# Windowed attention with a top-128 expert: ranking products at the ends of steps, loads two tiles ahead, weights a step later, batch entry behind the last turn

## The chip, the core and the metric

The kernel runs on one core of a Trainium2 chip. The time is the device time of one execution in microseconds; shown are the median of the runs and the smallest and largest of them. One execution more is taken with the hardware profiler, and all rows below are of that one.

## What is computed

Eight batches of 576 tokens go through attention with 8 heads of 64, where a token sees itself and the 63 tokens before it. The result, 512 wide, then goes through one expert per batch: the 128 tokens with the highest gate score are taken, go through two matrix products (512 to 1024 to 512), are scaled by the sigmoid of their score and added to the output at their places. The reference, cut:

```python
scores = scale * np.matmul(q, k.transpose(0, 1, 3, 2))     # 8 batches, 8 heads, S=576, D=64
mask = (rel >= 0) & (rel < 64)
scores = np.where(mask, scores, -1000000000.0)
...
x = attn @ v                                               # as (8, 576, 512)
gate = np.einsum('bsd,d->bs', x, w_gate)
out = x.copy()
for b in range(8):
    top_idx = np.argpartition(-gate[b], 128)[:128]
    xe = x[b, top_idx]
    ye = np.maximum(xe @ w1, 0.0) @ w2
    out[b, top_idx] = x[b, top_idx] + 1 / (1 + np.exp(-gate[b, top_idx])) * ye
```

All matrix products are made in full float32 for the attention, and for the expert from a high and a low part of each operand (three products: high by high, low by high, high by low), so that a product is as exact as float32.

## The kernel before

**Steps.** The 72 windows of 64 tokens (9 for each batch) are worked in 36 tiles of two windows. One step of the main loop (L690) works on several tiles at once: it issues the loads of tile n+3 (`AHEAD`), the store of tile n-3, the scores of tile n (TensorE, L264, tiles `s`), the values of tile n-2 (TensorE, L310, `av`), the maxima of tile n (VectorE, L276) and its exponentials (ScalarE, L284, `p`, first half), the transposes of tile n-1 (TensorE, L292, `t`) with their copies into `pt` (ScalarE, L294), the second half of the exponentials, and the output and gate dot of tile n-2 (VectorE, L319 to L322 and L237, `x` and `jk`; the dot lands in one column of `scores`). Each engine works off its instructions in the order in which they are written, so the order of the code is the order of the work.

**The expert stream.** `moe()` is a generator that issues one expert product or so each time it is asked. A step asks it `QUANTA` = 8 times, behind all of the step's attention. It goes through the batches in groups, (0), (1), (2), (3), (4, 5), (6, 7). For a single batch: `moe_in` transposes the 128 gathered rows `xe` (TensorE, `xt`, L501) and splits them into `xh` and `xl` (ScalarE copies, VectorE subtracts, L226 and L227); 24 products N=512 against `w1` give `hp` (L581) in two halves; the halves `n` are turned (TensorE, `ht`, L557; turn 0 and turn 1) and split into `hh` and `hl`; 24 products against `w2` give `yp` (L632), which is scaled, added (L638) and scattered by an indirect DMA on GpSimd's queue (L641). A pair has its products N=256 in the other orientation (`hp` L598) and no turn. While `yp` of a batch is being made the next group may enter: at column c in `ENTER` = (3, 6), if the rows have been gathered (L620). When the attention is through, a tail loop (L736) asks the stream `TAILQ` = 6 times behind each point of the ranking.

**The ranking.** `choose(b)` is a generator for each batch that a step advances at named points (`step_chain`). It transposes the gate scores of the batch's tiles into rows (`r`, TensorE, L409; the first four tiles as one part, the fifth as the other), copies the row (ScalarE, L413), counts for each token how many are larger (VectorE, five compares, `cmp`, L421), sums up where the chosen ones go (`lo`, 15 products N=1, L446), makes `diff` (L455), selects by slot (`sel`, L462: five instructions on GpSimd, on VectorE for the batches 0 and 7, which are called urgent), and sums up the indices (`ix`, five products, L471). `fx` and `idx` (VectorE, L475 and L477) and an indirect DMA (L479) gather the rows. The points of a step were, in this order: F, scores, values, P, maxima and first exponentials, S, R, transposes, output and gate, V, expert stream, E.

**Buffers in PSUM.** Two for the scores (`ps_s`), two for the transposes `t`, and for `r`, `lo` and `ix` as well (`ps_t`), one for the values, two for the expert stream's `hp`, `ht`, `yp` and `xt` (`ps_m`). In the tail the stream takes from `ps_t` too, once no ranking is left.

**Weights.** The 16 pieces of `w1` and `w2` are loaded by `load_w` in the steps of `PIECES`, and split into high and low on GpSimd (L207, L209) `WLAG` = 3 steps later, behind the step's V point. **Dummy products.** `keep_warm` (L95, `kw`) puts groups of four 64-wide products on zeros behind the scores of steps 0 to 2, 8, 6 and 3 groups.

Of the kernel before, what the change touches and what calls it, by code (L numbers as in the profile page):

```python
# [24 lines left out]
AHEAD = 3  # L25
# [7 lines left out]
KEEP = {0: 8, 1: 6, 2: 3}  # L33
# [3 lines left out]
PIECES = {n: 1 for n in range(2, 10)} | {10: 2, 11: 1, 12: 2, 13: 2, 14: 1}  # L37
WLAG = 3
# [3 lines left out]
ENTER = (3, 6)  # L42
# [7 lines left out]
def tile_attention_moe(ctx: ExitStack, tc, q, k, v, wg, w1, w2, outs, B, H, S, D, C):  # L50
# [44 lines left out]
    def keep_warm(groups):  # L95

        d = [ps_m.tile([P, 512], F32, tag="x", name=f"kw{r}_{njunk[1]}") for r in range(2)]
        njunk[1] += 1
        for i in range(groups):
            for r, c in ((0, 0), (1, 1), (0, 1), (1, 0)):  # L100
                rs = slice(r * W, (r + 1) * W)
                nc.tensor.matmul(d[r][c * W:(c + 1) * W, :D1], warm[rs, c * W:(c + 1) * W],
                                 warm[rs, :D1], start=True, stop=True)

# [240 lines left out]
    closed = set()  # L347
# [46 lines left out]
    def choose(b):  # L394
# [31 lines left out]
        for part, (t0, t1) in enumerate(CUT):  # L426
            yield "P"
            while (b, part) not in closed:
                yield "P"
            yield from spread(t0, t1)  # L430
            if urgent:
                yield "V"
                for t in range(t1):
                    compare(t, t0 * P, min(end, t1 * P), part)
# [5 lines left out]
        yield "P"  # L440

# [15 lines left out]
        for t, (_, r, lo, _) in enumerate(segs):  # L457
# [4 lines left out]
            (nc.vector if urgent else nc.gpsimd).tensor_scalar(  # L462
# [3 lines left out]
        yield "E" if urgent else "P"  # L466
        while b - 4 >= scattered[0]:
            yield "P"
# [47 lines left out]
    def moe():  # L516
        for gi, group in enumerate(GROUPS):
# [94 lines left out]
            for u, b in enumerate(group):  # L612
# [4 lines left out]
                for c in range(KC2):  # L617
                    if ng == 1 and c == 4:
                        yield from turn_done(1)
                    if c in ENTER and u == ng - 1 and gi + 1 < len(GROUPS):  # L620
                        nxt = [x for x in GROUPS[gi + 1] if x not in entered]
                        if nxt and is_ready(nxt[0]):
                            moe_in(gi + 1, GROUPS[gi + 1].index(nxt[0]))
                            yield
                            yield
# [28 lines left out]
    load_v(0)  # L654
    load_v(1)
    load_q(2)
    load_k(2)
    nc.sync.dma_start(wgb, wg)
    load_v(2)
# [30 lines left out]
    for n in range(NM + 3):  # L690
# [7 lines left out]
        if 0 <= n - 3 < NM:  # L698
            attn_store(n - 3)
        step_chain("F")  # L700
        if n < NM:
# [5 lines left out]
        step_chain("P")  # L707
# [3 lines left out]
        step_chain("S")  # L711
        step_chain("R")
# [5 lines left out]
        if 0 <= n - 2 < NM:  # L718
            attn_out(n - 2)
            attn_gate(n - 2)  # L720
            for b in range(B):
                for part, (_, t1) in enumerate(CUT):
                    if SEG[b][t1 - 1][0] == n - 2:
                        closed.add((b, part))
# [11 lines left out]
    while chains or not done:  # L736
        slot += 1
        for kind in ("F", "P", "S", "R", "V", "E"):
# [40 lines left out]
```

## Time and profile before

| what | value |
|---|---|
| time, median of 3 runs | 279.59 us (277.85 to 279.79) |
| profiled execution | 277.96 us |
| its span, from first to last instruction | 276.15 us |
| mean granted clock of TensorE | 0.967 |
| busy: TensorE, VectorE, ScalarE, GpSimd | 238.1, 186.5, 152.7, 80.9 us |
| DMA, mean | 171 GB/s |

An engine that is busy for the whole span would have 276 us in the third row from below. The granted clock is the share of full speed that the chip gave TensorE. In a list of waits, "PE t L292 <- ACT row L413" means that TensorE stood idle in front of the product on line 292 that writes `t`, until ScalarE had ended the instruction on line 413 that writes `row`.

### The profile page before, as it was taken

The page shows a single profiled execution, that of the slowest core. Times are in us where ns is not written, and L with a number is a line of the kernel's source. Part 1 is how long each engine was busy: PE and PEld are TensorE (multiplying, and loading weights), DVE is VectorE, ACT ScalarE, POOL GpSimd, SP SyncE. Part 2 cuts the span into 40 slices and gives each one's busy share as a digit, 9 for nine tenths or more (in the row PEclk, how much of TensorE's full clock was granted, in tenths as well). Part 3 has the DMA queues.
Part 4 walks back from the last instruction along what each step waited for, and adds up shares of the span by engine and source line. Part 5 has one row for each costly group of instructions (what it writes and reads, how often), then busy time and mean ns, then how long its engine had stood idle before and what let it go on. Part 6 is the DMA issues. An engine that isn't in the chain of part 4 may idle for free.

```text
span 276.1 us, 11136 instructions
## 1 busy us (share of the span) xinstructions
PE 238.1 (86%) x4512; PEld 202.8 (73%) x4512; DVE 186.5 (68%) x959; ACT 152.7 (55%) x423; POOL 80.9 (29%) x123
## 2 busy tenths in 40 slices
PE   8885879879978898977979994999898799999992
PEld 8774668768765786766758883887686699879981
DVE  1596999999958896895638878495499744423321
ACT  2886777958766577683537876365668201122200
POOL 7225302970398515100520050105300520111011
PEclk9999988999999999995999999799999979999999
DMA  6999896997865387373556665262311220111011
GB/s 215 397 354 350 271 327 216 330 395 250 278 170 188 135 246 237 123 226 116 174 171 196 195 229 193 59 211 81 78 40 45 76 68 10 38 40 38 0 40 38
DMA packets 25156, 47.27 MB, mean 171 GB/s; under 512 B 2961, under 2 KB 3985, under 8 KB 25105
## 3 DMA queue, kind: packets, MB, share of 16 engines
q1 hardware_dynamic: 23680, 42.10, 46.0%
q0 software_dynamic: 1280, 4.20, 4.5%
q8 instruction: 36, 0.59, 0.9%
q10 hardware_dynamic: 144, 0.26, 0.3%
q14 instruction: 16, 0.12, 0.2%
HBM read 35.01 MB, written 11.53 MB: 169 GB/s over the span
## 4 chain that ended last, share of the span: by engine, by line
PE 46%; issue 17%; DVE 16%; ACT 13%; POOL 6%; POOLq 0%; ACTq 0%; DVEq 0%
PE s L264 10%; PE t L292 10%; PE av L310 8%; ACT p L284 7%; PE yp L632 6%; PE hp L581 5%; DVE p L276 5%; PE hp L598 3%; ACT pt L294 3%; DVE jk L237 2%; DVE x L322 2%; DVE cmp L421 2%; POOL sel L462 2%; DVE hl L227 1%; PE wp L93 1%
## 5 line engine op out<-in xcount | busy, mean ns | idle before, releaser
L284 ACT ACTIVATE p<-p,nm 128x128 f32<-128x128 f32 x288 | 91.7, 392 | 42.6 <-DVE nm L276 41.1
L276 DVE CUSTOM_DVE_ANT_0 p<-s,mask 128x128 f32<-128x128 f32 x288 | 63.5, 285 | 26.8 <-PE s L264 24.1
L292 PE MATMUL t<-ident,p 128*128 128x128 f32 x288 | 42.1, 281 | 13.1 <-ACT row L413 9.6
L310 PE MATMUL av<-v,pt 64*64 64x65 f32 x2176 | 44.7, 226 | 7.1 <-issue 5.9
L294 ACT COPY pt<-t 128x512 f32<-128x512 f32 x72 | 40.0, 583 | 19.1 <-PE t L292 18.9
L310 PEld LDWEIGHTS av<-v,pt 64*64 64x64 f32 x2176 | 42.2, 140 | 9.3 <-issue 7.3
L292 PEld LDWEIGHTS t<-ident,p 128*128 128x128 f32 x288 | 31.1, 141 | 19.3 <-ACT row L413 12.1
L264 PE MATMUL s<-k,q 64*64 64x128 f32 x1152 | 43.3, 286 | 1.3 <-DVE nm L276 0.5
L264 PEld LDWEIGHTS s<-k,q 64*64 64x64 f32 x1152 | 33.7, 139 | 12.6 <-issue 11.4
L462 POOL TENSOR_SCALAR sel<-slots,diff 128x128 bf16<-128x128 f32 x24 | 18.5, 781 | 40.2 <-DVE z L319 39.5
L237 DVE CUSTOM_DVE_ANT_0 jk<-x,wgb 128x512 bf16<-128x512 f32 x36 | 28.4, 789 | 1.2
L632 PE MATMUL yp<-w2h,hh 128*128 128x512 f32 x64 | 27.5, 430 | 0.3 <-POOL w2h L207 0.3
L632 PE MATMUL yp<-w2l,hh 128*128 128x512 f32 x64 | 26.2, 410 | 1.2 <-POOL w2l L209 1.2
L632 PE MATMUL yp<-w2h,hl 128*128 128x512 f32 x64 | 26.2, 410 | 0.0
L421 DVE SCALAR_TENSOR_TENSOR cmp<-row,scores,later 128x128 bf16<-128x128 f32 (+12 forms) x48 | 25.4, 561 | 0.5 <-ACT row L413 0.4
L322 DVE TENSOR_TENSOR x<-av,z 128x512 f32<-128x512 f32 x36 | 24.9, 691 | 1.2
L641 POOL DMA_INDIRECT out_dram<-xe,idx x8 | 8.2, 1020 | 58.6 <-DVE xe L638 48.1
L276 DVE DVE_READ_ACCUMULATOR2_ANT nm<- 128x1 f32 x288 | 23.7, 82 | 0.0
L479 POOL DMA_INDIRECT xe<-out_dram,idx x8 | 8.3, 1038 | 45.7 <-DVE nm L276 24.5
L598 PE MATMUL hp<-xh,w1l 128*128 128x256 f32 x64 | 18.4, 288 | 0.0
L598 PE MATMUL hp<-xh,w1h 128*128 128x256 f32 x64 | 18.3, 286 | 0.0
L598 PE MATMUL hp<-xl,w1h 128*128 128x256 f32 x64 | 18.3, 286 | 0.0
(84 smaller groups left out, 324.5 us busy)
## 6 DMA issues: line engine op xcount, KB each, us to landing
v<-in_v SPq DMA_DIRECT2D x36, 260.0 KB, 3.6
q<-in_q SPq DMA_DIRECT2D x36, 256.0 KB, 4.0
out_dram<-x SPq DMA_DIRECT2D x32, 256.0 KB, 2.8
k<-in_k SPq DMA_DIRECT2D x31, 256.0 KB, 4.2
st<-in_w SPq DMA_DIRECT2D x16, 256.0 KB, 4.6
k<-in_k SPq DMA_DIRECT2D x8, 128.0 KB, 3.2
out_dram<-x SPq DMA_DIRECT2D x8, 128.0 KB, 2.4
k<-in_k ACTq DMA_DIRECT2D x1, 256.0 KB
```

Source lines behind the costliest of these rows:

```text
L237: nc.vector.tensor_tensor_reduce(out=junk()[:n, :E], in0=xf[:n], in1=wgb[:n], op0=ALU.mult, op1=ALU.add, scale=1.0, scalar=0.0, accum_out=acc)
L264: nc.tensor.matmul(s[r][c * W:(c + 1) * W, j], Q[m][rs, j, c], keys(m, c, j, rs), start=True, stop=True)
L276: nc.vector.tensor_tensor_reduce(out=pe[:, j, :, r], in0=s[r][:, j], in1=mk, op0=ALU.add, op1=ALU.min, scale=-SCALE, scalar=3.0e38, accum_ ...
L284: nc.scalar.activation(pe[:, j, :, r], pe[:, j, :, r], AF.Exp, bias=nm[:, r, j:j + 1], scale=-1.0)
L292: nc.tensor.transpose(t[:, j, :], pe[:, j, a].rearrange("p r w -> p (r w)"), ident)
L294: nc.scalar.copy(pt, t)
L310: nc.tensor.matmul(av[cs, r, j * D1:(j + 1) * D1], pt[a][rs, j, cs], V[g // 2][rs, g % 2, j], start=a == 0 or o == c, stop=a == 1)
L322: nc.vector.tensor_tensor(out=x.rearrange("p j r d -> p r j d"), in0=av[:, :, :, :D], in1=z[:, 1].unsqueeze(3).to_broadcast([P, 2, NP, D]) ...
L421: nc.vector.scalar_tensor_tensor(out=above[t][r, c0:c1], in0=row[r, c0:c1], scalar=scores[r, m:m + 1], in1=later[r, c0 - a:c1 - a], op0=AL ...
L462: (nc.vector if urgent else nc.gpsimd).tensor_scalar(out=sel[r], in0=slots[r], scalar1=diff[r, t:t + 1], scalar2=float(lo - r.start), op0= ...
L598: nc.tensor.matmul(hp[:, j], w[:, c, js], a[:, c].rearrange("p u c -> p (u c)"), start=(n == 0), stop=(n == 3 * KC1 - 1))
L632: nc.tensor.matmul(yp[:C, :E], a[:, c % per, us], w[:, c, :], start=(n == 0), stop=(n == 3 * KC2 - 1))
```

## The change

- `r`, `lo` and `ix` are written at E, behind a step's expert products, and no more at P, ahead of its transposes. A part is taken only when its last gate dot was written in an earlier step (`closed` now holds the step). Their readers (row copy at R, indices at F, selections at S) stand first in the next step, ahead of its scores. Batches that are not urgent wait at one V more between the last compare and `lo`.
- The selections of batch 1 go from GpSimd to VectorE.
- Loads run two tiles ahead, no more three; `wgb` is loaded between the values of tiles 0 and 1.
- `keep_warm(n)` issues one product of n times 128 columns, n = 2, 2, 1 in the steps 0 to 2, in place of 32, 24 and 12 small ones.
- The weights' first piece is loaded in step 3, no more in 2, and split two steps later, no more three. The loads end in step 15.
- The next group enters at any column from 3 on, but behind a single batch only when both turns were made in an earlier block (a block is one step's share of the stream).
- The tail loop has R ahead, and no P.

```diff
-AHEAD = 3
+AHEAD = 2
...
-KEEP = {0: 8, 1: 6, 2: 3}
-PIECES = {n: 1 for n in range(2, 10)} | {10: 2, 11: 1, 12: 2, 13: 2, 14: 1}
-WLAG = 3
+KEEP = {0: 2, 1: 2, 2: 1}
+PIECES = {n: 1 for n in range(3, 16)} | {9: 2, 13: 2, 14: 2}
+WLAG = 2
...
-ENTER = (3, 6)
+ENTER = (3, 4, 5, 6, 7)
...
-    def keep_warm(groups):
-        d = [ps_m.tile([P, 512], F32, tag="x", name=f"kw{r}_{njunk[1]}") for r in range(2)]
+    def keep_warm(n):
+        d = ps_m.tile([P, 512], F32, tag="x", name=f"kw{njunk[1]}")
         njunk[1] += 1
...
+        nc.tensor.matmul(d[:, :n * P], warm, warm.unsqueeze(1).to_broadcast([P, n, P]),
+                         start=True, stop=True)
...
         for part, (t0, t1) in enumerate(CUT):
-            yield "P"
-            while (b, part) not in closed:
-                yield "P"
+            yield "E"
+            while (b, part) not in closed or closed[b, part] >= slot:
+                yield "E"
             yield from spread(t0, t1)
...
                 compare(t, 0, end, 0)
-        yield "P"
+            yield "V"
+        yield "E"
...
-            (nc.vector if urgent else nc.gpsimd).tensor_scalar(
+            (nc.vector if urgent or b == 1 else nc.gpsimd).tensor_scalar(
...
-        yield "E" if urgent else "P"
+        yield "E"
         while b - 4 >= scattered[0]:
-            yield "P"
+            yield "E"
...
-                    if c in ENTER and u == ng - 1 and gi + 1 < len(GROUPS):
+                    if (c in ENTER and u == ng - 1 and gi + 1 < len(GROUPS)
+                            and (ng > 1 or len(turned) == 2 and turned[1] < block[0])):
...
+    nc.sync.dma_start(wgb, wg)
     load_v(1)
-    load_q(2)
-    load_k(2)
-    nc.sync.dma_start(wgb, wg)
-    load_v(2)
...
+        step_chain("R")
         step_chain("F")
+        step_chain("S")
         if n < NM:
             attn_scores(n)
...
-        step_chain("P")
         if n < NM:
             attn_max(n)
             attn_exp(n, 0)
-        step_chain("S")
-        step_chain("R")
...
-                        closed.add((b, part))
+                        closed[b, part] = n
...
-        for kind in ("F", "P", "S", "R", "V", "E"):
+        for kind in ("R", "F", "S", "V", "E"):
```

The change moves instructions on every engine. Three places show how. A row is a line of the code, what it does, what it writes and what it reads; the number behind a name is the buffer.

**The ranking of batch 3 in step 19.** On TensorE before, `r3_0`, the transposed gate scores of the first four tiles of batch 3, stood ahead of the step's transposes `t18`, and batch 1's expert products behind these:

```order
L409 MATMUL r3_0_2390<-ident_162,scores_184 128x128 x4
L292 MATMUL t18_0_2421<-ident_162,p18_2264 128x128 x4
L292 MATMUL t18_1_2428<-ident_162,p18_2264 128x128 x4
L581 MATMUL hp1_0_2306<-w1h_186,xl1_2199 128x512
L581 MATMUL hp1_0_2306<-w1h_186,xh1_2198 128x512
L581 MATMUL hp1_0_2306<-w1l_187,xh1_2198 128x512
```

After, the transposes stand earlier in the step, and `r3_0` behind the last of its eight expert products, right ahead of the scores of step 20:

```order
L575 MATMUL hp1_0_2329<-w1h_186,xl1_2218 128x512
L575 MATMUL hp1_0_2329<-w1h_186,xh1_2217 128x512
L575 MATMUL hp1_0_2329<-w1l_187,xh1_2217 128x512
L403 MATMUL r3_0_2338<-ident_162,scores_184 128x128 x4
L258 MATMUL s20_0_2352<-k4_1867,q20_2117 64x128
L258 MATMUL s20_1_2353<-k4_1867,q20_2117 64x128
```

On ScalarE before, at the ranking of batch 4 in step 24, the row copy stood between the first half of the step's exponentials (`p24`, four of them) and the copies `pt23` of the transposes:

```order
L284 ACTIVATE p24_3003<-p24_3003,nm24_3004 128x2x64 x4
L413 COPY row4_2933<-r4_0_2998 128x512
L294 COPY pt23_0_3023<-t23_0_3018 128x512
L294 COPY pt23_1_3030<-t23_1_3025 128x512
L284 ACTIVATE p24_3003<-p24_3003,nm24_3004 128x2x64 x4
```

After, it stands ahead of the step's exponentials, which are those of tile 25 there, behind the last of the step before and its split of batch 2's rows:

```order
L278 ACTIVATE p24_2876<-p24_2876,nm24_2877 128x2x64 x4
L220 CAST xh2_2915<-xt2_2917 128x512
L407 COPY row4_2810<-r4_0_2946 128x512
L278 ACTIVATE p25_3022<-p25_3022,nm25_3023 128x2x64 x4
L288 COPY pt24_0_3041<-t24_0_3036 128x512
L288 COPY pt24_1_3048<-t24_1_3043 128x512
L278 ACTIVATE p25_3022<-p25_3022,nm25_3023 128x2x64 x4
```

**The entry of batch 2.** On TensorE before, in step 22, `ht1_1` (the second turn of batch 1) and `xt2` (the entry of batch 2) stood in one step with three products between them:

```order
L292 MATMUL t21_0_2762<-ident_162,p21_2634 128x128 x4
L292 MATMUL t21_1_2769<-ident_162,p21_2634 128x128 x4
L557 MATMUL ht1_1_2788<-ident_162,n1_1_2677 128x128 x4
L632 MATMUL yp1_2684<-w2h_188,hh1_0_2561 128x512
L632 MATMUL yp1_2684<-w2l_189,hh1_0_2561 128x512
L632 MATMUL yp1_2684<-w2h_188,hl1_0_2562 128x512
L501 MATMUL xt2_2802<-ident_162,xe2_2581 128x128 x4
L632 MATMUL yp1_2684<-w2h_188,hh1_0_2561 128x512
```

After, the turn stands in step 22, behind its transposes,

```order
L286 MATMUL t22_0_2785<-ident_162,p22_2657 128x128 x4
L286 MATMUL t22_1_2792<-ident_162,p22_2657 128x128 x4
L551 MATMUL ht1_1_2812<-ident_162,n1_1_2700 128x128 x4
L627 MATMUL yp1_2707<-w2h_188,hh1_0_2578 128x512
L627 MATMUL yp1_2707<-w2l_189,hh1_0_2578 128x512
```

and the entry in step 23, behind that step's transposes, with all of the step's attention between the two:

```order
L286 MATMUL t23_0_2890<-ident_162,p23_2771 128x128 x4
L286 MATMUL t23_1_2897<-ident_162,p23_2771 128x128 x4
L495 MATMUL xt2_2917<-ident_162,xe2_2604 128x128 x4
L627 MATMUL yp1_2707<-w2h_188,hh1_1_2817 128x512
L627 MATMUL yp1_2707<-w2l_189,hh1_1_2817 128x512
L627 MATMUL yp1_2707<-w2h_188,hl1_1_2818 128x512
```

**The tail.** On TensorE before, in step 36, the entry of batch 4 stood behind the transposes and three products of batch 3's `yp`; the second turn of batch 3, `ht3_1`, had come a step earlier:

```order
L292 MATMUL t35_1_4393<-ident_162,p35_4295 128x128 x4
L632 MATMUL yp3_4336<-w2h_188,hh3_0_4228 128x512
L632 MATMUL yp3_4336<-w2l_189,hh3_0_4228 128x512
L632 MATMUL yp3_4336<-w2h_188,hl3_0_4229 128x512
L501 MATMUL xt4_4414<-ident_162,xe4_3671 128x128 x4
```

After, the second turn comes behind the values of tile 35; `r7_0` and the entry of batch 4 follow four products later, and the entry of batch 5 three products behind that:

```order
L551 MATMUL ht3_1_4375<-ident_162,n3_1_4317 128x128 x4
L627 MATMUL yp3_4324<-w2h_188,hl3_0_4250 128x512
L627 MATMUL yp3_4324<-w2h_188,hh3_0_4249 128x512
L627 MATMUL yp3_4324<-w2l_189,hh3_0_4249 128x512
L627 MATMUL yp3_4324<-w2h_188,hl3_0_4250 128x512
L403 MATMUL r7_0_4388<-ident_162,scores_184 128x128 x4
L495 MATMUL xt4_4401<-ident_162,xe4_3685 128x128 x4
L627 MATMUL yp3_4324<-w2h_188,hh3_1_4380 128x512
L627 MATMUL yp3_4324<-w2l_189,hh3_1_4380 128x512
L627 MATMUL yp3_4324<-w2h_188,hl3_1_4381 128x512
L495 MATMUL xt5_4411<-ident_162,xe5_4150 128x128 x4
```

On VectorE before, the split of that turn (`hl3_1`) stood ahead of the output and gate dot (`x34`, `jk39`) of the last tile but one:

```order
L237 ISA jk38_4332,scores_184<-x33_4328,wgb_185 128x512
L237 ISA scores_184 128x1
L421 SCALAR_TENSOR_TENSOR cmp0_2_200,cnt2_194<-row6_4005,scores_184,later_167 128x320
L421 SCALAR_TENSOR_TENSOR cmp0_3_201,cnt2_194<-row6_4005,scores_184,later_167 128x192
L227 TENSOR_TENSOR hl3_1_4343<-ht3_1_4337,hh3_1_4342 128x512
L319 TENSOR_SCALAR z34_4400<-av34_4353 128x8
L321 RECIPROCAL z34_4400<-z34_4400 128x8
L322 TENSOR_TENSOR x34_4401<-av34_4353,z34_4400 128x2x4x64
L237 ISA jk39_4405,scores_184<-x34_4401,wgb_185 128x512
L237 ISA scores_184 128x1
L421 SCALAR_TENSOR_TENSOR cmp0_4_202,cnt2_194<-row6_4005,scores_184,later_167 64x64
L227 TENSOR_TENSOR xl4_4413<-xt4_4414,xh4_4412 128x4x128
```

After, it stands behind the output and gate dot (`x35`, `jk40`) of the last tile, and four compares of batch 7 stand between it and the splits of the two entries:

```order
L315 RECIPROCAL z35_4367<-z35_4367 128x8
L316 TENSOR_TENSOR x35_4368<-av35_4334,z35_4367 128x2x4x64
L231 ISA jk40_4372,scores_184<-x35_4368,wgb_185 128x512
L231 ISA scores_184 128x1
L415 SCALAR_TENSOR_TENSOR cmp0_4_202,cnt2_194<-row6_3890,scores_184,later_167 64x64
L221 TENSOR_TENSOR hl3_1_4381<-ht3_1_4375,hh3_1_4380 128x512
L415 SCALAR_TENSOR_TENSOR cmp1_0_203,cnt3_196<-row7_4314,scores_184,later_167 64x448
L415 SCALAR_TENSOR_TENSOR cmp1_1_204,cnt3_196<-row7_4314,scores_184,later_167 128x384
L415 SCALAR_TENSOR_TENSOR cmp1_2_205,cnt3_196<-row7_4314,scores_184,later_167 128x256
L415 SCALAR_TENSOR_TENSOR cmp1_3_206,cnt3_196<-row7_4314,scores_184,later_167 128x128
L221 TENSOR_TENSOR xl4_4400<-xt4_4401,xh4_4399 128x4x128
L221 TENSOR_TENSOR xl4_4400<-xt5_4411,xh4_4399 128x4x128
```

## Rows read from the trace of the kernel before

**Rows 1.** The page, busy time of TensorE with its share of the span, and the granted clock in 40 slices (tenths of full speed).

```profile
PE 238.1 (86%) x4512; PEld 202.8 (73%) x4512; DVE 186.5 (68%) x959; ACT 152.7 (55%) x423; POOL 80.9 (29%) x123
PEclk9999988999999999995999999799999979999999
```

**Rows 2.** The chain that ended last, in order of time, over steps 12 and 13: start in us, length in us, engine, what.

```profile
60.60 1.03 PE s L264 x32
61.64 0.93 PE av L310 x64
62.57 1.02 PE t L292 x8
63.59 1.86 PE hp L581 x8
65.45 1.03 PE s L264 x32
```

**Rows 3.** Windows over the whole span, cut where step 0, step 10, step 35, the first product of the pair (4, 5) and the end of TensorE's work (270.87) lie: window, its length, then busy us (and number) of TensorE, its weight loads, VectorE, ScalarE, GpSimd; granted clock, DMA share, GB/s.

```profile
4.82:47.84 43.02, 34.61 (x1035) 30.68 (x1034) 34.73 (x219) 31.93 (x94) 12.84 (x34) 0.96 0.93 320
47.84:204.14 156.30, 136.27 (x2847) 112.83 (x2847) 118.44 (x625) 103.05 (x288) 53.59 (x58) 0.97 0.59 190
204.14:222.61 18.47, 15.79 (x303) 13.30 (x303) 16.09 (x68) 8.73 (x22) 3.91 (x5) 0.94 0.16 59
222.61:270.87 48.26, 47.70 (x317) 42.50 (x315) 16.30 (x47) 7.73 (x20) 5.95 (x6) 0.99 0.10 34
```

**Rows 4.** TensorE's waits between 48 and 204 us: engine, instruction and line that waited, <- the releaser; us in total, times, longest.

```profile
PE t L292 <- ACT row L413: 7.0, 9, 1.7
PE xt L501 <- DVE hl L227: 5.7, 2, 3.3
PE t L292 <- ACT pt L294: 2.9, 4, 0.7
PE yp L632 <- POOL w2l L209: 1.2, 1, 1.2
```

**Rows 5.** Windows over steps 3 to 5, steps 6 to 9, and step 12 alone, columns as in rows 3.

```profile
15.35:29.64 14.29, 9.83 (x313) 8.70 (x313) 11.36 (x64) 10.25 (x31) 6.75 (x7) 1.00 1.00 335
29.64:47.84 18.20, 15.41 (x427) 13.63 (x426) 17.68 (x106) 14.22 (x42) 2.28 (x2) 0.91 0.82 275
60.53:65.38 4.85, 4.85 (x113) 4.15 (x113) 4.73 (x24) 2.81 (x10) 0.46 (x1) 1.00 0.84 286
```

**Rows 6.** TensorE's waits between 0 and 48 us, and the dummy products (durations in ns, smallest, median, longest; first and last start).

```profile
PE av L310 <- issue: 4.5, 3, 2.7
PE t L292 <- ACT row L413: 2.6, 2, 1.7
...
L102 PE MATMUL kw<-warm x136: 216/218/253, 6.0 to 13.2; 64*64 64x65 f32 x136
```

**Rows 7.** The chain in step 24, where a ranking product stands ahead of the transposes.

```profile
135.91 1.28 ACT p L284 x4
137.20 0.59 ACT row L413
...
137.84 0.67 PE t L292 x4
```

**Rows 8.** The selections, by engine: durations in ns, smallest, median, longest; first and last start.

```profile
L462 POOL TENSOR_SCALAR sel<-slots,diff x24: 712/718/1328, 74.5 to 218.2; 128x128 bf16<-128x128 f32 x24
L462 DVE TENSOR_SCALAR sel<-slots,diff x8: 278/284/288, 43.4 to 229.4; 128x128 bf16<-128x128 f32 x8
```

**Rows 9.** VectorE's gate dots over all tiles (times, busy us, mean ns), then rows of VectorE's timeline: one gate dot, and compares of the last batch (start, length, line, tiles).

```profile
L237 DVE CUSTOM_DVE_ANT_0 jk<-x,wgb 128x512 bf16<-128x512 f32 x36 | 28.4, 789 | 1.2
...
53.38 1.56 DVE L237 CUSTOM_DVE_ANT_0 jk<-x,wgb 128x512 bf16<-128x512 f32 x1
...
217.72 0.69 DVE L421 SCALAR_TENSOR_TENSOR cmp<-row,scores,later 64x448 bf16<-64x448 f32 x1
...
219.39 0.36 DVE L421 SCALAR_TENSOR_TENSOR cmp<-row,scores,later 128x128 bf16<-128x128 f32 x1
...
221.96 0.35 DVE L421 SCALAR_TENSOR_TENSOR cmp<-row,scores,later 128x128 bf16<-128x128 f32 x1
```

**Rows 10.** The entry of batch 2 in step 22, rows of the timeline (start, length; in brackets the idle time of the engine before), and windows over step 22, step 23 and step 29, columns as in rows 3.

```profile
125.13 0.69 DVE L227 TENSOR_TENSOR hl<-ht,hh 128x512 fp32r<-128x512 f32 x1 [0.49 <-ACT hh L226]
125.88 1.12 PE L501 MATMUL xt<-ident,xe 128*128 128x128 f32 x4 [3.28 <-DVE hl L227]
...
118.41:127.35 8.94, 5.66 (x117) 4.68 (x117) 6.51 (x34) 5.73 (x17) 0.00 (x0) 0.86 0.70 231
127.35:134.43 7.08, 7.08 (x129) 6.32 (x128) 4.43 (x23) 3.75 (x11) 2.32 (x4) 0.69 0.25 78
164.63:175.06 10.43, 6.71 (x107) 5.15 (x106) 6.59 (x29) 5.47 (x16) 1.26 (x2) 0.89 0.42 148
```

**Rows 11.** TensorE's timeline at the entry of batches 6 and 7, and TensorE's waits behind step 35's start.

```profile
242.92 0.60 PE L501 MATMUL xt<-ident,xe 128*128 128x128 f32 x4
...
246.18 0.63 PE L501 MATMUL xt<-ident,xe 128*128 128x128 f32 x4 [0.56 <-issue]
...
PE ix L471 <- POOL sel L462: 0.9, 2, 0.5
PE ix L471 <- POOL selh L462: 0.8, 1, 0.8
```

More of the change, by code (lines that the diff above doesn't have):

```diff
@@ L93, in tile_attention_moe @@
         nc.tensor.matmul(wp[:, j % NP], warm, warm, start=True, stop=True)
-    def keep_warm(groups):
-        d = [ps_m.tile([P, 512], F32, tag="x", name=f"kw{r}_{njunk[1]}") for r in range(2)]
+    def keep_warm(n):
+        d = ps_m.tile([P, 512], F32, tag="x", name=f"kw{njunk[1]}")
         njunk[1] += 1
[L99 to L103, printed above, removed]
+        nc.tensor.matmul(d[:, :n * P], warm, warm.unsqueeze(1).to_broadcast([P, n, P]),
+                         start=True, stop=True)
     FILL = -1e9 / SCALE
@@ L346, in tile_attention_moe @@
     scattered = [0]
-    closed = set()
+    closed = {}
     def segments(b):
```

## The prediction

> **What bounds the kernel now.** I read the page first: TensorE is busy for 238.1 us of a span of 276.1, far more than any other engine, and its clock stands below full in a few slices [rows 1]. Then I read the chain over two steps in which nothing is late: one step repeats after 4.85 us (60.60 to 65.45), and all of it is TensorE: scores 1.03, values 0.93, transposes 1.02, eight expert products 1.86 [rows 2]. So 2.98 us of attention and 0.233 us for each N=512 product are the prices, and a step that takes longer has a wait in it. Third, I cut the span where steps begin [rows 3]: the start (4.82 to 47.84, steps 0 to 9) takes 43.02 us, the middle (steps 10 to 34) 156.30 with TensorE busy for 136.27, the last attention step with all up to the first product of the pair (4, 5) 18.47 with 15.79 busy, the paired products 48.26 with 47.70 busy; from there to the end of the span, 276.15, it is 5.28. The middle holds 20.0 us of idle TensorE, which the list of its waits names almost whole [rows 4]: transposes behind the ranking's row copy 7.0, and 2.9 behind the `pt` copy that the first wait delays; the entry of a batch behind a split 5.7; `yp` behind weight splits 1.2. The start has other limits: VectorE is busy for 17.68 of the 18.20 us of steps 6 to 9 [rows 5], and its largest TensorE wait, 4.5 us before `av`, shows no releaser [rows 6].
>
> **The ranking products.** Before, `r` stands in front of a step's transposes, and it takes one of the two `ps_t` buffers that they need. Its reader, the row copy on ScalarE, stands behind the four exponentials: exponentials from 135.91, row copy at 137.20, transposes only at 137.84 [rows 7]. In the change `r`, `lo` and `ix` follow the step's expert products, and the readers are the first in the next step, ahead of exponentials and maxima. The next transposes come 1.96 us into the step (scores and values), and the row copy is by then done. I take back the 7.0 and the 2.9 of the middle whole: a step without ranking waits for nothing there. The waits in the start (2.6 us) [rows 6] I count at nothing, since VectorE is full there.
>
> What is added: `lo`, `ix` and `r` now stand ahead of the next scores, so a late one holds the step's scores, and VectorE and ScalarE behind these. `r` needs a gate dot of the step before and no more than a `pt` copy's buffer. `lo` has a free step behind the last compare, but for batches 0 and 7. `ix` waits for five selections on GpSimd, begun at the step's start: five at the median 0.718 are 3.6 us, at the longest 1.328 6.6 us [rows 8], against 4.7 us of TensorE work ahead of `ix`. I take 1.0 for the four batches in the middle (bounds 0 and 4 times 1.9). Batch 0's `lo` waits for compares of the same step: scores 9 start after VectorE has ended step 8, which leaves it idle for `lo` and what the selections don't cover; I take 1.0 of bounds 0 and 3.
>
> **Batch 1's selections** go from GpSimd to VectorE: 5 at 0.284 for batches 0 and 7 [rows 8], 1.4 us in step 16, where TensorE has 5.2 us of work; on the path nothing. VectorE does run longer beside GpSimd: a gate dot took 1.56 us at 53.38 against a mean of 0.789 [rows 9], so up to twice the 1.4. [...]
>
> **Entry behind the last turn.** In steps 22 and 29 the next batch's transposes `xt` follow the turn `ht` in the same step and need its PSUM buffer, so TensorE waits until ScalarE and then VectorE (125.13) have split it, to 125.88 [rows 10]: 5.7 us in two places. The change lets a batch enter only in a later step, after 3 us of that step's attention, when the split is done. Behind both waits the granted clock falls: 0.86 over 8.94 us, 0.69 over the next 7.08, 0.89 over 10.43 [rows 10]. At half speed these are 2.5, 4.4 and 2.3 us, together 9.2, of which about 1.0 idle; the busy rest costs half, 4.1 us. I take 5.7 and 4.1 (below: 5.7 alone).
>
> **Weights a step later.** The first use is a step later too (the expert stream starts in step 12 and no more in 11), and w2's pieces are split one step ahead of their product; GpSimd is rid of batch 1's selections. I take the 1.2 us [rows 4].
>
> **Two tiles ahead, fewer dummy products.** The 136 records of `kw` end at 13.2 us [rows 6]; nothing but tiles that VectorE holds back waits behind them, so they are worth 0 to 0.5. Fewer loads are queued in the first 15 us. Whether the 4.5 us without a releaser come from full queues the trace doesn't say; I take 2.0 back, of bounds 0 and 4.5. A load still has about three steps, some 14 us, ahead of its use.
>
> **The tail pays.** The expert stream is a step behind, and six products and one turn (1.4 + 0.5 us) move from the middle behind step 35's scores. Now turn 1 of batch 3 stands behind the last `av`, and batch 4 enters a step after it. Its buffer is free when VectorE has split the turn, and this split stands behind the last tile's output, gate dot and compare. From the start of step 35's scores TensorE needs 1.03 + 0.93 + 1.02 + 0.5 + 1.4 + 0.93 + 1.02 + 1.86 + 0.93 + 0.5 + 0.93 + 0.5 = 11.6 us to `xt4`. VectorE was busy for 16.1 us in this stretch before [rows 3]; of that, two splits of `xt` (0.69 each), four compares of batch 7 (217.72 to 219.75, 2.0) and five narrow ones (0.35 each) [rows 9, 10] now stand behind turn 1's split, and 11.0 ahead of it. It starts with the end of the scores at 1.1 and loses some 0.5 to batch 3's gate, which goes over ScalarE: 12.6 at the best. I allow it another 0.5, so 1.5 of wait (bounds 1.0 and the longest wait of an entry before, 3.3). Then `xt5` comes only three products after `xt4`, 1.2 us on, and needs the same buffer, whose split stands behind the four compares, 2.7: 1.5 more. Such holes lowered the clock twice before, so I add one drop of 3.4 us at half speed (half of the first one's 6.9), 1.7. Further on `xt7` comes three products after `xt6`, before it was nine; 242.92 to 246.18 is the turnaround of its buffer [rows 11], 3.3, less 0.5 and 0.7: a wait of 2.1 in place of 0.56. The wait for batch 6's selections (0.9 + 0.8) [rows 11] moves into the paired products and has a scatter ahead of it on GpSimd; I take 2.2. One more drop of the clock there, 1.7.
>
> **The sum,** against the profiled execution's own span: before step 0 4.8. Start 43.0 - 2.0 + 1.0 = 42.0. Middle 156.3 - 9.9 - 5.7 - 4.1 - 1.2 - 1.9 (moved) = 133.5, and 1.0 for `ix` and 2.0 for steps in which VectorE, busy for 118 us of then some 134, becomes the longer one: 136.5. To the first paired product: 15.8 busy, less 1.1 for its own half clock (0.94 over 18.47), plus 1.9 + 1.5 + 1.5 + 1.7 = 21.3. Paired products 48.3 - 0.5 (half clock) - 0.6 + 2.1 + 2.2 + 1.7 = 53.2. End 5.3. Together 263.1. The profiled execution took 277.96 us, 1.81 more than its span, and the median of the runs lies 1.63 above it: 266.5 us.
>
> **The rivals.** *The tail doesn't stall:* VectorE has no backlog, no clock drops follow. Then 1.5 + 1.5 + 3.4 us less: 260. For it speaks that VectorE's steps 33 and 34 are light; against it that the split stands behind the last gate in any case. Chance 0.18. *VectorE takes half of it:* removed waits gave it time to catch up; half of 9.9 + 5.7 stays as waits of scores for maxima: 274. For it speaks that it would be busy for 118 of some 136 us in the middle; against it that the step of [rows 2] keeps its 4.85 us with VectorE at work for nearly all of it. Chance 0.13. *No clock at the start:* without the dummies TensorE runs steps 2 to 9 at half clock; a step's 2.98 us become 5.96 where 4.6 are taken now (18.20 over four steps [rows 5]), 8 times 1.3 is 10.4: 277. Against it: steps 3 to 5 had no dummies and a granted clock of 1.00 at 9.83 us busy of 14.29 [rows 5]. [...] Chance 0.05. *The change does little:* each wait returns in front of the scores, 277 to 281, chance 0.06. *Slower:* GpSimd's selections take 1.33 each; `ix` holds the scores for 1.9 us and the clock falls behind it for 1.7 each time, 3.6 in four steps of the middle, and 1.9 more in the tail: 16.3, so 283. It loses to the kernel before once each of the four costs over 2.8. Chance 0.06.
>
> **The numbers.** The forecast itself, 261 to 272, has 0.52. About 1% is what a measurement of this kernel can tell, 276.8 to 282.4: faster 0.83, the same 0.11, slower 0.06. The range 257 to 277 leaves out the lower edge of the first rival and the last three.
>
> **What would show it.** Right: no transposes behind a row copy; steps of 4.9 to 5.6 us through the middle, which then takes about 136; `xt2` and `xt3` without a wait and no half clock there; a wait of 1 to 3 us before `xt4` and one before `xt5`. Wrong: scores that wait for maxima in most steps; `ix` waiting for GpSimd over 1 us in each batch; a clock below full before 30 us; a start of over 45 us.

## The result and the profile after

The changed kernel takes **264.15 us** (median of 4 runs, 263.02 to 264.91), the kernel before 279.44 (277.85 to 279.79): a ratio of 0.946, interval 0.9405 to 0.9515. Ratios and intervals, here and below, compare only the faster runs of the two kernels, so that they can differ from the ratio of the medians beside them. The profiled execution took 264.91 us with a span of 263.1, the span of the forecast. Its parts did not all come out so.

The page of the changed kernel, busy times and granted clock in 40 slices, as in [rows 1]:

```profile
PE 237.1 (90%) x4382; PEld 203.7 (77%) x4382; DVE 186.8 (71%) x964; ACT 149.2 (57%) x423; POOL 74.4 (28%) x118
PEclk9999998999999999999999999999995979979999
```

TensorE is busy for nearly as long as before, in a span that is 13 us shorter. Its clock is full from the 8th to the 30th slice, where before it fell twice, and it falls three times in the tail. The windows of the changed kernel, cut at the same events and with the columns of [rows 3] (line numbers of the changed kernel are some 5 or 6 lower: L495 is `xt`, L627 `yp`, L440 `lo`, L465 `ix`):

```profile
4.81:49.24 44.43, 35.12 (x905) 30.26 (x904) 36.56 (x224) 32.47 (x96) 13.68 (x35) 0.96 0.92 312
49.24:181.44 132.20, 128.05 (x2837) 109.06 (x2836) 116.23 (x623) 99.12 (x286) 45.52 (x50) 1.00 0.68 221
181.44:203.47 22.03, 19.16 (x307) 15.62 (x307) 14.84 (x59) 8.63 (x22) 1.06 (x1) 0.86 0.17 56
203.47:257.83 54.36, 51.09 (x322) 45.29 (x320) 18.21 (x58) 7.71 (x20) 9.55 (x11) 0.93 0.09 30
```

| stretch | before | forecast | changed |
|---|---|---|---|
| start, steps 0 to 9 | 43.02 | 42.0 | 44.43 |
| middle, steps 10 to 34 | 156.30 | 136.5 | 132.20 |
| step 35 to the first paired product | 18.47 | 21.3 | 22.03 |
| paired products | 48.26 | 53.2 | 54.36 |
| end | 5.28 | 5.3 | 5.28 |

The middle gives 24.1 us and was to give 19.8; the tail takes 9.7 of that back, and 7.8 was forecast; the start takes 1.4 where it was to give 1.0. TensorE's waits in the middle of the changed kernel (49 to 181.5 us), beside [rows 4]:

```profile
PE av L304 <- issue: 1.2, 3, 0.4
PE r L403 <- ACT pt L288: 1.0, 3, 0.5
PE s L258 <- DVE z L313: 0.7, 2, 0.5
PE ix L465 <- POOL sel L456: 0.7, 1, 0.7
```

No transposes stand behind a row copy or a late `pt`, no entry behind a split, no `yp` behind a weight split. ScalarE's timeline shows why the first is gone. The row copy of batch 4 stands at 129.04, ahead of step 25's exponentials, and the transposes of that step come at 130.1:

```profile
128.58 0.57 ACT L220 CAST xh<-xt 128x512 fp32r<-128x512 f32 x1
129.04 0.59 ACT L407 COPY row<-r 128x512 f32<-128x512 f32 x1
130.18 0.99 ACT L278 ACTIVATE p<-p,nm 128x128 f32<-128x128 f32 x3 [0.55 <-DVE nm L270]
```

The waits that came in the start and in the tail, from TensorE's waits of 0 to 48 and of 181.4 to 264 us:

```profile
PE av L304 <- issue: 2.7, 3, 1.1
PE lo L440 <- DVE z L315: 2.6, 1, 2.6
PE lo L440 <- DVE cmp L415: 1.3, 1, 1.3
...
PE xt L495 <- issue: 1.9, 1, 1.9
PE xt L495 <- DVE xl L221: 1.3, 1, 1.3
PE xt L495 <- DVE hl L221: 1.2, 1, 1.2
PE ix L465 <- POOL sel L456: 0.8, 2, 0.5
PE ix L465 <- POOL selh L456: 0.5, 1, 0.5
```

From below: five selections of batch 6 on GpSimd, `xt4`, `xt5` and `xt7`, each at the place that the prediction named. The timeline of the tail shows the order behind the first two. Turn 1's split (`hl`) stands behind the last gate dot and holds `xt4`; the compares of batch 7 stand ahead of `xl`, and `xl` holds `xt5`:

```profile
193.79 0.69 DVE L231 CUSTOM_DVE_ANT_0 jk<-x,wgb 128x512 bf16<-128x512 f32 x1
...
194.62 0.68 DVE L221 TENSOR_TENSOR hl<-ht,hh 128x512 fp32r<-128x512 f32 x1
195.33 0.69 DVE L415 SCALAR_TENSOR_TENSOR cmp<-row,scores,later 64x448 bf16<-64x448 f32 x1
195.35 0.66 PE L495 MATMUL xt<-ident,xe 128*128 128x128 f32 x4 [1.21 <-DVE hl L221]
...
197.26 0.68 DVE L221 TENSOR_TENSOR xl<-xt,xh 128x512 fp32r<-128x512 f32 x1
198.00 1.12 PE L495 MATMUL xt<-ident,xe 128*128 128x128 f32 x4 [1.29 <-DVE xl L221]
```

The drops of the clock in the tail, as windows (columns as in [rows 3]): 6.8, 3.4 and 3.5 us at a granted clock of 0.50, 0.50 and 0.51, in which TensorE is busy for 13.2. At half speed they cost half of that by my estimate, 6.6 us together.

```profile
197.50:204.30 6.80, 6.30 (x33) 5.22 (x34) 1.72 (x3) 0.85 (x2) 0.00 (x0) 0.50 0.00 0
211.20:214.60 3.40, 3.40 (x18) 3.40 (x17) 1.09 (x5) 0.60 (x1) 0.01 (x1) 0.50 0.00 0
231.60:235.10 3.50, 3.50 (x10) 2.72 (x9) 0.87 (x3) 0.77 (x3) 0.00 (x0) 0.51 0.02 5
```

### The profile page after: what moved, and what is told of

Same layout as the page of the kernel before. It is cut to its first block, busy times and chain, and to the rows that moved or that the text cites. A ratio compares the mean times of both kernels' runs of the same rounds, so it can differ in the third digit from the quotient of the medians.

```text
span 263.1 us, 10857 instructions
## 1 busy us (share of the span) xinstructions
PE 237.1 (90%) x4382; PEld 203.7 (77%) x4382; DVE 186.8 (71%) x964; ACT 149.2 (57%) x423; POOL 74.4 (28%) x118
## 4 chain that ended last, share of the span: by engine, by line
PE 47%; DVE 21%; issue 17%; ACT 8%; POOL 4%; POOLq 1%; ACTq 0%; DVEq 0%
PE s L258 11%; PE av L304 9%; PE t L286 7%; DVE p L270 5%; PE yp L627 5%; PE hp L575 5%; DVE cmp L415 5%; ACT p L278 5%; PE hp L592 4%; DVE jk L231 3%; DVE x L316 3%; ACT pt L288 2%; POOL sel L456 2%; PE r L403 1%; PE wp L93 1%
## 5 line engine op out<-in xcount | busy, mean ns | idle before, releaser
L304 PE MATMUL av<-v,pt 64*64 64x65 f32 x2176 | 43.8, 223 | 4.3 <-issue 4.3
L304 PEld LDWEIGHTS av<-v,pt 64*64 64x64 f32 x2176 | 40.9, 137 | 6.9 <-issue 5.8
L288 ACT COPY pt<-t 128x512 f32<-128x512 f32 x72 | 37.9, 575 | 5.2 <-PE t L286 5.2
L286 PE MATMUL t<-ident,p 128*128 128x128 f32 x288 | 39.3, 280 | 0.3 <-DVE fx L469 0.3
L627 PE MATMUL yp<-w2h,hh 128*128 128x512 f32 x64 | 27.8, 434 | 0.0
L627 PE MATMUL yp<-w2h,hl 128*128 128x512 f32 x64 | 26.9, 420 | 0.0
L627 PE MATMUL yp<-w2l,hh 128*128 128x512 f32 x64 | 26.8, 419 | 0.0
L456 POOL TENSOR_SCALAR sel<-slots,diff 128x128 bf16<-128x128 f32 x20 | 14.3, 722 | 27.7 <-DVE diff L449 27.1
L600 ACT ACTIVATE hh<-hp 128x512 fp32r<-128x512 f32 x8 | 4.8, 597 | 29.0 <-PE hp L592 29.0
L592 PE MATMUL hp<-xl,w1h 128*128 128x256 f32 x64 | 19.0, 297 | 0.0
L601 DVE SCALAR_TENSOR_TENSOR hl<-hp,hh 128x512 fp32r<-128x512 f32 x8 | 5.5, 691 | 19.0 <-ACT hh L600 19.0
```

The costliest lines, as they stand in the source:

```text
L286: nc.tensor.transpose(t[:, j, :], pe[:, j, a].rearrange("p r w -> p (r w)"), ident)
L288: nc.scalar.copy(pt, t)
L304: nc.tensor.matmul(av[cs, r, j * D1:(j + 1) * D1], pt[a][rs, j, cs], V[g // 2][rs, g % 2, j], start=a == 0 or o == c, stop=a == 1)
L456: (nc.vector if urgent or b == 1 else nc.gpsimd).tensor_scalar(out=sel[r], in0=slots[r], scalar1=diff[r, t:t + 1], scalar2=float(lo - r.st ...
L592: nc.tensor.matmul(hp[:, j], w[:, c, js], a[:, c].rearrange("p u c -> p (u c)"), start=(n == 0), stop=(n == 3 * KC1 - 1))
L627: nc.tensor.matmul(yp[:C, :E], a[:, c % per, us], w[:, c, :], start=(n == 0), stop=(n == 3 * KC2 - 1))
```

## The experiments

Three sets of four ran, each set on one chip beside the kernel before, with six runs of each kernel and eleven of the one before. My theory: the ranking's place and the entry rule carry the gain, loads and weights a little, and the tail gives back what its waits and their clock cost. The main rival: VectorE is the bound behind TensorE, so that a wait which is removed returns in front of the scores.

**One part alone, on the kernel before.** The ranking's edits:

```diff
-            yield "P"
-            while (b, part) not in closed:
-                yield "P"
+            yield "E"
+            while (b, part) not in closed or closed[b, part] >= slot:
+                yield "E"
...
+        step_chain("R")
         step_chain("F")
+        step_chain("S")
```

> The kernel before with only the ranking moved (r, lo, ix at E, readers first in a step, the free V ahead of lo, batch 1's selections on VectorE, the tail's order of points). By my theory the waits of transposes behind the row copy and the pt copy (9.9 us in the middle, 2.6 in the start) go, the wait of lo for batch 0's compares (3.9, as in the changed kernel) comes, and some 2 us of waits of r and ix; entry waits and their half clock stay: 279.4 - 12.5 + 3.9 + 1.9 = 272 to 273. By the rival, that VectorE or the scores take up half of what the transposes gave back, 277 to 278.

The entry rule:

```diff
-ENTER = (3, 6)
+ENTER = (3, 4, 5, 6, 7)
...
+                            and (ng > 1 or len(turned) == 2 and turned[1] < block[0])):
```

> The kernel before with only the entry rule. By my theory the two entry waits (5.7) and the half clock behind them (4.1) go, and the tail pays 1.3 for xt5 three products behind xt4, 1.4 more for xt7 three behind xt6, and one drop of the clock (1.7): 279.4 - 9.8 + 4.4 = 274. By the rival, that the clock falls for the ranking's waits in any case, the 4.1 stay: 278. If the tail doesn't stall: 270.

The loads, and the weights:

```diff
-AHEAD = 3
+AHEAD = 2
```

> The kernel before with only the loads two tiles ahead and the gate weights loaded between the values of tiles 0 and 1; dummy products as before. By my theory the waits of av without a releaser fall from 4.5 us to 2.7, as in the changed kernel: 277.6. By the rival, that these went for another reason (the dummies, the ranking, the weights a step later), 279.4.

```diff
-WLAG = 3
+WLAG = 2
...
-PIECES = {n: 1 for n in range(2, 10)} | {10: 2, 11: 1, 12: 2, 13: 2, 14: 1}
+PIECES = {n: 1 for n in range(3, 16)} | {9: 2, 13: 2, 14: 2}
```

> The kernel before with only the weights' steps (first piece in step 3, split two steps later). By my theory the 1.2 us of yp behind a split stay or go with the step in which they are split, and nothing else changes: 278.2 if they go. By the rival, that the expert stream, which is not a step later here, then waits longer for splits, 280 to 282.

| kernel | median us (range) | ratio to before (interval) |
|---|---|---|
| before, beside them | 278.29 (273.59 to 280.07) | |
| ranking alone | 271.16 (268.76 to 273.33) | 0.9824 (0.9715 to 0.9933) |
| entry alone | 273.53 (271.06 to 276.58) | 0.9882 (0.9774 to 0.9989) |
| loads alone | 280.85 (277.47 to 283.53) | 1.0136 (1.002 to 1.0252) |
| weights alone | 278.9 (277.39 to 280.74) | 1.0116 (1.0025 to 1.0207) |

The first two times agree with my theory (272 to 273, and 274). For the entry rule this is in part luck: its middle gave 5.5 us where 9.8 was expected, and its tail took 1.4 (68.1 against 66.7) where 4.4 was. TensorE's waits in the middle, of the ranking alone, then of the entry rule alone:

```profile
PE xt L502 <- DVE hl L227: 7.0, 2, 3.7
```

```profile
PE t L292 <- ACT row L413: 6.4, 9, 1.5
PE t L292 <- ACT pt L294: 2.9, 4, 0.7
```

Each part removes its own waits and leaves the other's. In the two kernels the middle takes 143.65 and 150.78 us, so 12.7 and 5.5 less than before (of the 12.7, some 3 is half clock: one drop, 3.4 us at 0.50, in place of two, the first of them, 6.8 us, twice as long); that is 18.2 of the 24.1 that all parts together give. For the clock the rival of the second run was right: the entry rule alone has three drops in the middle (granted clock 0.50 over 3.4 us each), and they follow a weight split (1.2 us of wait at 89.1), a late transpose (1.5 at 127.1) and a row copy (188.7). Windows ahead of two of them, and in them:

```profile
87.60:91.00 3.40, 1.88 (x13) 0.89 (x16) 3.15 (x6) 1.12 (x4) 3.32 (x3) 1.00 0.76 269
91.00:94.40 3.40, 3.40 (x97) 3.28 (x90) 1.85 (x17) 1.28 (x4) 1.48 (x2) 0.50 0.02 5
...
186.60:190.00 3.40, 2.17 (x40) 1.55 (x37) 3.26 (x21) 1.84 (x5) 1.35 (x2) 1.00 0.02 5
190.00:193.40 3.40, 3.40 (x12) 2.82 (x12) 0.05 (x1) 2.83 (x7) 1.06 (x1) 0.50 0.62 154
```

Loads and weights alone take no time off; both ratios stand a little over 1. With the loads alone the waits of `av` without a releaser are 4.0 us in the start, where my theory had 2.7. The weights alone still show `yp` behind its split (L209) for 1.2 us, the ranking alone does not.

**The tail and batch 0, on the changed kernel.** Batch 6's selections on VectorE. In the changed kernel `ix` waits 1.3 us for them on GpSimd, and the granted clock is 0.50 from 211.20 to 214.60. My theory: both the wait and the 1.7 us of half clock go, 264.2 - 1.3 - 1.7 = 261.2.

```diff
-            (nc.vector if urgent or b == 1 else nc.gpsimd).tensor_scalar(
+            (nc.vector if urgent or b in (1, 6) else nc.gpsimd).tensor_scalar(
```

> The changed kernel with batch 6's selections on VectorE. [...] By the rival, that the narrow products of lo7 and ix6 themselves let the clock fall, the half clock stays: 262.9.

A pair's entries further apart:

```diff
-                            and (ng > 1 or len(turned) == 2 and turned[1] < block[0])):
+                            and (c in (3, 6) if ng > 1 else len(turned) == 2 and turned[1] < block[0])):
```

> The changed kernel with the entries of a pair at columns 3 and 6 only, so that xt7 stands nine products behind xt6 and not three. By my theory its wait falls from 1.9 us to about 0.5, and the half clock behind it at 230 to 234 us (1.7) goes: 264.2 - 1.4 - 1.7 = 261.1. By the rival, that the clock falls there in any case, 262.8.

The Relu with its last product:

```diff
                             n += 1
-                            yield
+                            if n < 3 * KC1:
+                                yield
                     h = p_h.tile([P, 512], F32, tag="h", name=f"n{gi}_{nb}")
...
                     nat.append((h, block[0]))
+                    yield
```

> The changed kernel with the Relu of a half written together with its last product, without a pause of the stream between them, so that the second turn of batch 3 stands ahead of the values of tile 35 and its split ahead of the last gate dot. By my theory xt4's wait of 1.2 us goes, xt5 keeps about 1.0 (three products behind xt4, its buffer's turnaround), and the half clock of 198 to 204 us (3.0) goes or is halved: 264.2 - 1.5 - 1.5 to 3.0 = 260 to 261. By the rival, that VectorE's backlog holds xt4 whatever the order, 264.

A free V for batch 0:

```diff
+        elif b == 0:
+            yield "V"
         yield "E"
```

> The changed kernel with one free V for batch 0 as well, so that its lo stands at the end of step 9 and no scores wait for its compares; the expert stream then starts one step later. By one theory the 3.9 us of lo's waits and the half clock behind them (1.7) are lost time, and 1.9 of products move to the tail: 264.2 - 5.6 + 1.9 = 260.5. By the rival, that VectorE is the bound of steps 6 to 9 and the wait only lies where VectorE is busy, the start gains at most 1.0 and the tail pays 1.9: 265.

| kernel | median us (range) | ratio to before (interval) | to the first pair | paired products |
|---|---|---|---|---|
| changed | 264.15 (263.02 to 264.91) | 0.946 (0.9405 to 0.9515) | 22.03 | 54.36 |
| selections of 6 | 259.96 (257.87 to 265.7) | 0.9484 (0.9351 to 0.9618) | 19.67 | 49.08 |
| pair's entries | 258.46 (257.37 to 263.81) | 0.9436 (0.9343 to 0.953) | 19.67 | 51.35 |
| Relu | 260.34 (259.82 to 261.9) | 0.9534 (0.9449 to 0.9619) | 18.18 | 50.31 |
| batch 0 | 268.88 (266.58 to 269.41) | 0.9808 (0.9705 to 0.9912) | 24.84 | 51.40 |

The row of the changed kernel is that of the result, from another set of runs. The first three intervals overlap the changed kernel's, so their times alone decide nothing. The profiles show that each wait went as expected: with the selections moved no `ix` waits in the tail, with the entries apart `xt7` waits 0.6 in place of 1.9, with the Relu early `xt4` waits no more and `xt5` keeps 1.2. What they don't show is that these waits set the clock: in the first, the holes ahead of `xt5` and `xt7` are the old ones (1.29 and 1.96 us), and the clock stays full behind both:

```profile
198.00:201.00 3.00, 1.71 (x22) 1.12 (x21) 1.87 (x7) 0.94 (x2) 0.00 (x0) 1.00 0.00 0
...
226.00:230.00 4.00, 3.83 (x21) 3.33 (x22) 1.62 (x6) 1.07 (x4) 0.00 (x0) 1.00 0.01 4
```

The last run came out worse than both theories. The start gains 0.7 and no more (43.70 against 44.43), since TensorE then waits 2.4 us ahead of the later `lo`; and this 0.7 is no gain, for the half clock at that wait (47.4 to 54.4 us) now falls mostly into the middle (mean granted clock 0.99 in the start, 0.98 in the middle, where the changed kernel has 0.96 and 1.00). The middle is 5.4 longer (137.55 against 132.20): 5.9 us of it run at half clock, and `hp` waits 2.2 for the split of batch 0's rows. The stream a step later costs 2.8 before the paired products, where 1.9 was expected. Waits of this kernel from 4.8 to 90 us:

```profile
PE lo L442 <- ACT pt L288: 2.4, 1, 2.4
PE hp L577 <- DVE xl L221: 2.2, 1, 2.2
```

**The cures together, and the small parts undone.** The three edits of the tail in one kernel, with a second entry behind a single batch at column 6 at the earliest:

```diff
+                            and (c in (3, 6) if ng > 1 else len(turned) == 2 and turned[1] < block[0]
+                                 and (c >= 6 or gi + 1 not in XT))):
```

> The changed kernel with three edits together: batch 6's selections on VectorE, the entries of a pair at columns 3 and 6 (and a second entry behind a single batch at column 6 at the earliest), the Relu of a half written with its last product. By my theory the tail's waits add up, so the cures do: start 45 and middle 133 as in the last runs, 17.9 from step 35 to the first paired product, 47.7 for the paired products: 4.8 + 45 + 133 + 17.9 + 47.7 + 5.3 + 1.8 = 255.5. By the rival, that one cure takes the place of the others (the cause is one late stream), 258 to 260.

```diff
-AHEAD = 2
+AHEAD = 3
...
-KEEP = {0: 2, 1: 2, 2: 1}
+KEEP = {0: 8, 1: 6, 2: 3}
```

> The changed kernel with the loads three tiles ahead, their order and the dummy products of the kernel before. By the prediction's step the start takes 2.0 us longer: 266. By the rival, that the loads and dummies are worth nothing here (the loads alone took no time off the kernel before), 264.

```diff
-WLAG = 2
+WLAG = 3
```

> The changed kernel with the weights' steps of before. By the prediction's step 1.2 us of yp behind splits come back: 265.4. By the rival, that these waits went with the ranking (the ranking alone shows none), nothing changes: 264.2.

> The changed kernel once more, beside the three others, for its spread: 264.2 if the half clock behind the tail's waits falls in each execution; 258 to 264 if the same waits lower the clock in one execution and not in another, as the profiles with the same waits and a full clock suggest.

| kernel | median us (range) | ratio to before (interval) |
|---|---|---|
| before, beside them | 278.38 (273.95 to 281.41) | |
| cures together | 256.33 (255.32 to 258.44) | 0.9269 (0.9195 to 0.9342) |
| loads and dummies undone | 262.72 (260.65 to 264.47) | 0.9483 (0.9404 to 0.9563) |
| weights undone | 262.64 (262.23 to 263.97) | 0.9496 (0.9432 to 0.956) |
| changed, again | 261.89 (258.02 to 264.6) | 0.9392 (0.9285 to 0.9499) |

The cures go together: 256.33, where 255.5 was expected, and of the tail's waits only 0.6 before `xt7` and 0.4 before `av` are left. Their times don't simply add up: against 264.15 the single cures gave 4.2, 5.7 and 3.8, and together they give 7.8; but the changed kernel's own runs already spread over 6.9 us (258.02 to 264.91). No clock drop is left behind step 10. Its windows for the middle, to the first paired product, and the paired products:

```profile
49.41:183.79 134.38, 128.65 (x2842) 109.78 (x2840) 117.13 (x622) 99.75 (x287) 45.74 (x50) 1.00 0.67 217
183.79:200.68 16.89, 16.34 (x303) 13.35 (x303) 14.88 (x59) 8.20 (x21) 1.06 (x1) 1.00 0.22 75
200.68:249.40 48.72, 47.87 (x321) 42.30 (x321) 19.04 (x63) 7.72 (x20) 5.93 (x6) 1.00 0.10 33
```

The tail now costs what it cost before the change (16.89 and 48.72 against 18.47 and 48.26), though it does more work. The middle is 2.2 longer than the changed kernel's; with the Relu's edit alone it is 134.27, so that this edit seems to cost something there. Undoing the loads with the dummies, or the weights, changes nothing that six runs can tell: both rivals. Nor do the profiles of the start. With the loads undone and in the changed kernel once more it differs by 0.6 us, at a granted clock of 0.89 and 0.93, and the waits of `av` without a releaser are nearly the same (columns as in [rows 3], then the waits):

```profile
4.54:51.82 47.28, 37.40 (x1035) 33.36 (x1034) 36.24 (x225) 32.39 (x95) 13.54 (x35) 0.89 0.90 310
4.81:51.52 46.71, 36.15 (x904) 31.02 (x904) 38.03 (x225) 32.59 (x96) 13.30 (x35) 0.93 0.88 297
...
PE av L310 <- issue: 4.5, 3, 2.7
PE av L304 <- issue: 4.0, 3, 1.5
```

The changed kernel once more came out at 258.02 to 264.6 us, as the second of its two expectations had it.

## Why the prediction came out

**The ranking products** were right: the 9.9 us of the middle are gone, with 0.9 for `ix` where 1.0 was taken, and the run with this part alone shows that it is this part. The scores don't take it back (0.7 us of waits for VectorE); the rival in which VectorE takes half is out.

**Batch 0's `lo`** was mis-sized: 1.0 with an upper bound of 3, measured 3.9. The step that failed reads "scores 9 start after VectorE has ended step 8, which leaves it idle": VectorE is not idle but works off its queue, 8.08 us of the 8.32 of step 8. This window of the changed kernel shows it:

```profile
35.95:44.27 8.32, 4.22 (x120) 3.60 (x120) 8.08 (x43) 4.85 (x16) 1.11 (x1) 0.98 1.00 331
```

So the wait lies where VectorE is the bound, and moving `lo` a step later gained nothing. On the other side the 2.6 us of transposes behind the row copy went, which the sum had left at nothing.

**Entry behind the last turn** was right in its waits (5.7 to 0). The 4.1 us of half clock are gone too, but the step that gives them to the entry fell: with the entry rule alone the clock fell three times in the middle, behind other waits (0.97 over the middle); in the changed kernel, where the row copies' waits are gone as well, it is 1.00. Nor is that half clock a fixed cost of the kernel before. Its 33 runs beside the experiments go from 281.4 us, at a mean granted clock of 0.967, down to 271.9 at 1.00. The gain doesn't hang on this: the longest run of the changed kernel, 264.91, is still shorter than 271.9. The clock is part of why the two parts together give more than the sum of each alone.

**Weights a step later:** the 1.2 us went, for another reason. The weights alone keep them, the ranking alone loses them, and without this part they don't come back. The ranking's edits also take batch 1's selections off GpSimd, where they stood for 4.5 us (73.6 to 78.1) ahead of the splits of w2, and with them alone the first product of `yp` comes at 81.4 us in place of 74.5. Which of the two gives the splits their time, the runs don't separate. **Batch 1's selections** cost 0.28 each on VectorE, as priced. GpSimd ran nothing between 74.4 and 88.9 us, so this run doesn't show what they cost beside a busy GpSimd; in the kernel before, the gate dots took 0.69 us where GpSimd was idle, and 0.69 to 1.62 where it ran. **Two tiles ahead, fewer dummy products:** the 2.0 us of the start are not shown. The wait without a releaser fell from 4.5 us to 2.7 in the changed kernel's first profile, but it was 4.0 in its second and 4.0 with the loads alone, and with the old loads 2.8 (ranking alone) and 4.5 (loads undone).

**VectorE's 2.0** for the middle came out as 0.7, the scores' waits for VectorE. TensorE is idle for 4.15 us there: besides the 0.7, it is 0.9 for `ix`, 1.2 before `av`, 1.0 for `r` behind a `pt` copy, which the sum had at nothing, and 0.3 before transposes. The forecast left 6.2 idle. With 2.2 us less of busy time than forecast this makes the middle 4.3 shorter than the sum had it. Of the 2.2 I can assign only some 0.6: before, the half clock behind the second entry lasted to 176.2, 1.1 us beyond the window that the prediction took.

**The tail** was right in place and size: waits of 1.2, 1.3 and 1.9 us where 1.5, 1.5 and 2.1 were taken, and 1.3 for the selections where 2.2 was. The mis-sized term is the clock: two drops of 1.7 were taken, three came, one of them twice as long, 6.6 us in place of 3.4. The rival that the tail doesn't stall is out. **No clock at the start** is out as well: the granted clock was 1.00 from 4.81 to 43 us, with TensorE busy for 29.6 of 38.2.

So the forecast's 263.1 is right in its main terms, and met the span exactly only because its errors cancel: the start 2.4 and the tail 1.9 too low, the middle 4.3 too high. The median came out 2.4 below the 266.5, because the sum put it 1.63 above the profiled execution, as it was before, and it lies 0.8 below.

## What to carry to other kernels

A producer that shares buffers and readers with the main loop belongs behind the step's other work, and its reader first in the next step; then its wait lies under a whole step (here 9.9 us of the transposes' waits went, and 0.9 for `ix` came). When such edits make a stream later, look at once at the end of the program, where nothing covers it: here the change gave 9.7 of 24.1 us back there, and three small edits of order brought the tail back to its length of before (65.6 against 66.7 us; the kernel takes 256.3). Price each wait of a bound engine also by what its clock does behind it, but as a chance and not as a certainty (here it fell to half behind a wait of 1.9 to 2.0 us before `xt7` in three profiles, and stayed full behind the same wait in two).

## What was not expected of the hardware

The same hole does not always lower TensorE's clock. Behind `xt7`'s wait of 1.9 to 2.0 us the granted clock fell to half in the changed kernel (0.51 over 3.5 us), with the weights undone (0.51 over 3.4 us) and with the loads undone, where the `yp` products behind it come every 0.43 us in place of 0.23. With batch 0's free V it is 0.96 over the paired products. It stayed full with batch 6's selections moved (1.00 from 226 to 230 us) and, by my estimate, with the Relu early: its paired products take 50.31 us, 1.2 more than the 49.08 of the former at 1.00, and 0.9 of that are waits of `ix`. In the changed kernel's second profile it stayed full as well, behind the same 1.95 us; this is the stretch in which the first profile has 0.51:

```profile
231.60:235.10 3.50, 3.47 (x18) 2.97 (x19) 1.19 (x5) 1.07 (x4) 0.00 (x0) 1.00 0.02 5
```

Behind the waits of `xt4` and `xt5` (1.2 and 1.3) it fell in the changed kernel's first profile (0.50 over 6.8 us) and with the weights undone (0.50 from 199.5 to 202.9 us), and stayed full with batch 6's selections moved (1.00 from 195 to 203.05 us). The changed kernel's runs, from 258.0 to 264.9 us, agree in size with such drops (1.7 to 3.4 us each); that they are the cause of that spread is argued, not shown. Why the same work met a full clock in one execution and half a clock in another, no run shows. What rid the kernel of the drops behind step 10 was to close the holes: with the cures together, 0.6 us before `xt7` and 0.4 before `av` are left, and the clock is 1.00 from 49.41 to 249.40.
